# A new order of all units, with named PSUM tiles and named evacuating engines, for a fused attention and gated MLP kernel

## The chip, the cores and the metric

The kernel runs on one core of one Trainium2 chip. The metric is device time in microseconds, of one execution; several executions are timed and their median is given. The profile is of one further execution.

Engines are named as in the profile: PE is TensorE's matmul row and PEld its weight loads, DVE is VectorE, ACT is ScalarE, POOL is GpSimd, SP is the engine that issues the remaining DMAs.

## The reference, cut to what matters

```python
B, H, S, D = 4, 8, 768, 64            # q, k, v;  sort_net is [B, H, 8, 8]
P = sort_net
for _ in range(5):                    # Sinkhorn: 8x8 mixing matrices
    P = exp(P - max(P));  P /= P.sum(-1);  P /= P.sum(-2)
k_sorted[b,h,i] = sum_j P[i,j] * k[b,h,j]      # blocks of 96 rows are mixed
v_sorted[b,h,i] = sum_j P[i,j] * v[b,h,j]
attn = softmax(q_block @ k_sorted_block.T / 8) # within each block of 96
x = (attn @ v_sorted_block)                    # -> [B, 768, 512]

h = relu(x @ w_in)                    # 512 -> 1024
u, v = h[..., :512], h[..., 512:]
v_n = (v - mean(v)) / sqrt(var(v) + 1e-6)
v_s = w_spatial @ v_n + b_spatial     # mixes the 768 positions
out = (u * v_s) @ w_out               # 512 -> 512, float32
```

## The kernel before, in words

Each batch is made of **units**. A unit is a group of matmuls or transposes into one PSUM tile (two banks, 4 KB a partition; four such tiles fill PSUM) and the instruction that empties the tile.

For the attention of one batch:

- `qtr(n)`, n = 0, 1: 24 transposes of q for four heads.
- `ktr(hp)`, hp = 0..3 (a pair of heads): 12 matmuls that mix k with the diagonal matrices `pdiag` and transpose it at once (`mixed_t`, line 274). `vtr(hp)` does the same with v, and `vblk(hp)` transposes that back into blocks of 96 rows; both are used for batch 0 alone.
- `vmix(hp)`: for batches 1 to 3, two matmuls that mix v. After two of them, half of the mixed v is stored to DRAM (`vd`) and read back in blocks (`vb`) by two DMAs on SP's queue.
- `score(n)`, n = 0..7 (pair of heads n // 2, half of the blocks n % 2): 8 matmuls, and the exponential on ACT (line 324).
- `attend(n)`: 8 matmuls, then reciprocal and multiplication on DVE (lines 347, 348) into `x_sb`.
- `xtr(n)`: 16 transposes of `x_sb` into `xt`.

For the gated MLP of one batch:

- `vproj(n)`, n = 0..2: 8 matmuls of 512 columns, relu on ACT (line 389), then on DVE the statistics of two groups of rows (lines 392, 393).
- `norm`: two ACT instructions on all variances, and six normalizations on DVE (line 403).
- `uproj(mc)`, mc = 0..3: 8 matmuls of 384 columns, relu on ACT (line 419).
- `wsp_unit(gs)`, gs = 0..5: six transposes of `w_spatial`, once in the kernel, copied by DVE.
- `spatial(mc)`: 12 matmuls of 384 columns (line 428), the addition of the bias on DVE (line 434, `vs`), and the product with u on GpSimd (line 438, `gt`); the last of all has that product on DVE.
- `oproj(n)`, n = 0..2: 8 matmuls of 512 columns (line 449), the copy on ACT, and a DMA of 512 KB to the output on SP's queue.

The order of PE, DVE, ACT and GpSimd is that of the program text (`tc.manual_schedule`), so each engine takes its instructions as written. The opening is: loads, Sinkhorn, `warm(4)` (four dummy matmuls of 512 columns), both `qtr` of batch 0, `spread(0, 1)` (turns the mixing matrices of batch 0 into columns on 128 partitions: matmuls, a copy, a matmul, a copy), `make_pdiag`, `warm(2)`, and then the string `order`, which is the attention of batch 0. One step of it, `spread`, does the same for the other three batches and lets GpSimd make their `pdiag`. Then comes a loop over the four batches with one string `steps`: the gated MLP of batch b, with the attention of batch b + 1 woven in. In each turn of the loop `load` issues the loads of q, k and v of batch b + 2 on GpSimd's queue, after a copy `gate` of one element of `vb`, which holds GpSimd until that transfer has landed.

`ps_tile` draws from a pool of four buffers under one tag, so the units take the four PSUM tiles in turn:

```python
psum = ctx.enter_context(tc.tile_pool(name="psum", bufs=4, space=bass.MemoryType.PSUM))
def ps_tile(dt=FP32):
    return psum.tile([128, 2, 512 if dt == FP32 else 1024], dt, name="ps", tag="ps")
```

A unit whose turn comes to a tile that is still being emptied waits, and all of PE's later units with it. Lines 217 and 219 are the copies of the helper `copy` on ACT and on DVE.

Of the kernel before, what the change touches and what calls it, by code (L numbers as in the profile page):

```python
# [29 lines left out]
def kernel(  # L30
# [12 lines left out]
    nc = tc.nc  # L43
# [25 lines left out]
    moe_pool = ctx.enter_context(tc.tile_pool(name="moe", bufs=5))  # L69
# [16 lines left out]
    nc.sync.dma_start(out=b_nat, in_=_raw_ap(moe_b_spatial, 0, [[0, 128], [1, S]]))  # L86
# [45 lines left out]
    nc.gpsimd.dma_start(out=w_in_sb, in_=moe_w_in.rearrange("(kc p) f -> p kc f", p=128))  # L132
    wsp_nat = pers.tile([128, G, S], BF16)
# [8 lines left out]
    mask_ps = ps_tile()  # L142
# [25 lines left out]
    def warm(n):  # L168
        t = ps_tile()
        for _ in range(n):  # L170
            nc.tensor.matmul(t[:, 0, :], lhsT=ident_bf, rhs=warm_sb, start=True, stop=True)
# [4 lines left out]
    def spread(b, nb):  # L176
        n = nb * NB * H
        pt_ps = ps_tile()
        for i in range(NB):
            nc.tensor.matmul(  # L180
                pt_ps[0:NB, 0, 0:n].rearrange("p (b i h) -> p b i h", i=NB, h=H)[:, :, i, :],
                lhsT=p_bf[:, i, :], rhs=ident_bf[0:BH, b * H:(b + nb) * H],
                start=True, stop=True,
            )
        pt_sb = small.tile([NB, B * NB * H], BF16, name="pt", tag="pt")
        nc.vector.tensor_copy(out=pt_sb[:, 0:n], in_=pt_ps[0:NB, 0, 0:n])
        prep_ps = ps_tile()
        nc.tensor.matmul(prep_ps[:, 0, 0:n], lhsT=sel16, rhs=pt_sb[:, 0:n], start=True, stop=True)
        nc.vector.tensor_copy(
            out=prep_sb[:, b:b + nb].rearrange("p b i h -> p (b i h)"), in_=prep_ps[:, 0, 0:n],  # L190
        )
# [13 lines left out]
    def wsp_unit(gs):  # L205
        tp = ps_tile(BF16)
# [6 lines left out]
        nc.vector.tensor_copy(out=wspT[:, gs, :], in_=tp[:, 0, 0:S])  # L213

    def copy(eng, out, in_):
        if eng is nc.scalar:
            nc.scalar.copy(out=out, in_=in_)  # L217
        else:
            nc.vector.tensor_copy(out=out, in_=in_)  # L219

# [3 lines left out]
    class Attention:  # L224
        def __init__(self, b):
# [3 lines left out]
            self.q, self.k, self.e, self.vT = {}, {}, {}, {}  # L229

        def vmix(self, hp, eng):
            t = ps_tile()
# [12 lines left out]
            if hp == 0:  # L245
                self.vb = att.tile([BLK, NB, 2, H // 2, VW], BF16, name="vb", tag="vb")
            if hp % 2 == 1:
# [7 lines left out]
        def qtr(self, n, eng):  # L255
            t = ps_tile(BF16)
# [13 lines left out]
        def mixed_t(self, src, hp, eng):  # L270
            t = ps_tile().rearrange("p x c -> p (x c)")
# [16 lines left out]
        def ktr(self, hp, eng):  # L288
            self.k[hp] = self.mixed_t(k_in, hp, eng)


        def vtr(self, hp, eng):
            self.vT[hp] = self.mixed_t(v_in, hp, eng)

        def vblk(self, hp, eng):
            half, h0 = hp // 2, 2 * hp % (H // 2)
            if hp == 0:
                self.vb = vb0
            t = ps_tile(BF16)
# [10 lines left out]
        def score(self, n):  # L310
            hp, ih = n // 2, n % 2
            t = ps_tile()
# [17 lines left out]
        def attend(self, n):  # L330
            hp, ih = n // 2, n % 2
            if n == 0:
                self.x = att.tile([BLK, NB, DM], BF16, name="x_sb", tag="x")
            t = ps_tile()
# [20 lines left out]
        def xtr(self, n, eng):  # L355
            t = ps_tile(BF16)
# [13 lines left out]
    class Gmlp:  # L370
        def __init__(self, b):
            self.b = b
            self.v, self.u, self.gt = [], {}, []
            self.xt = [xts[b, kc] for kc in range(KC)]

        def vproj(self, n):
            t = ps_tile()
# [8 lines left out]
            if n == 0:  # L386
                self.mv = small.tile([128, G, 2], FP32, name="mv", tag="mv")
            v_sb = vsb_pool.tile([128, 2, DH], BF16, name="v_sb", tag="v")
            nc.scalar.activation(out=v_sb, in_=t, func=AF.Relu)  # L389
            for x in range(2):  # L390
# [3 lines left out]
                self.v.append(v_sb[:, x, :])  # L394

        def norm(self):
# [12 lines left out]
        def uproj(self, mc):  # L409
            t = ps_tile()  # L410
            for kc in range(KC):
# [7 lines left out]
            nc.scalar.activation(  # L419
                out=u_sb.rearrange("p (x c) -> p x c", x=2), in_=t[:, :, 0:HW], func=AF.Relu,  # L420
            )
            self.u[mc] = u_sb

        def spatial(self, mc, eng):
            t = ps_tile()
# [16 lines left out]
            self.gt.append(gt)  # L442

        def oproj(self, n, eng):
            t = ps_tile()
            for mc in range(FC):
                for x in range(2):
                    g = 2 * n + x
                    nc.tensor.matmul(  # L449
                        t[:, x, :], lhsT=self.gt[mc][:, g * 128:(g + 1) * 128],  # L450
                        rhs=w_out_sb[:, mc, :],
                        start=(mc == 0), stop=(mc == FC - 1),
                    )
            o_sb = o_pool.tile([128, 2, DM], FP32, name="o_sb", tag="o")
            copy(eng, o_sb, t)
            nc.sync.dma_start(
                out=out[self.b].rearrange("(p g) n -> p g n", g=G)[:, 2 * n:2 * n + 2, :],
                in_=o_sb,
            )

    ACT, DVE = nc.scalar, nc.vector
    with tc.manual_schedule(engines={ET.PE, ET.DVE, ET.Activation, ET.Pool}):
        a = Attention(0)
# [6 lines left out]
        order = """  # L470
            ktr0A vtr0D ktr1A vtr1A score0 vblk0D score1 ktr2D attend0 score2 attend1 score3 vblk1D
            vtr2A attend2 ktr3A attend3 score4 spread vblk2D score5 attend4 vtr3A attend5 score6
            score7 vblk3D attend6 xtr0A attend7 xtr1D
        """
        for step in order.split():
            name, rest = step.rstrip("0123456789AD"), step.lstrip("abcdefghijklmnopqrstuvwxyz")
            if name == "spread":
                spread(1, 3)
                for b in range(1, B):
                    make_pdiag(b, nc.gpsimd, 0, H)  # L480
# [4 lines left out]
            else:  # L485
                getattr(a, name)(int(rest[0]), *[{"A": ACT, "D": DVE}[e] for e in rest[1:]])
        for b in range(B):
            m = Gmlp(b)
            last = b == B - 1
            a = None if last else Attention(b + 1)  # L490
            steps = """
                vproj0 vmix0 vproj1 vmix1 vmix2 vproj2 vmix3 qtr0 norm wsp0 uproj0 ktr0 ktr1 wsp1
                uproj1 qtr1 score0 score1 wsp2 uproj2 ktr2 ktr3 wsp3 load uproj3 score2 score3
                wsp4 wsp5 spatial0 attend0 attend1 score4 score5 spatial1 attend2
                attend3 spatial2 score6 score7 attend4 attend5 spatial3 attend6 attend7 xtr0
                oproj0 oproj1 xtr1 oproj2
            """.split()
            for step in steps:
# [56 lines left out]
```

## Time and profile before

| what | value |
|---|---|
| median of 3 runs | 190.55 us (190.03 to 192.42) |
| the profiled execution | 189.82 us |
| its span, first to last instruction | 188.1 us |
| mean granted TensorE clock | 0.961 |
| PE busy | 160.3 us (85% of the span) |
| DVE busy | 108.8 us (58%) |
| ACT busy | 82.5 us (44%) |
| POOL busy | 46.9 us (25%) |
| moved by DMA | 23.92 MB, 127 GB/s over the span |

In the groups of the profile, a line gives source line, engine, operation, output and inputs with their shapes and the number of instructions, then the busy time of all of them in us, the mean of one in ns, and the idle time of the engine just before them. In the chain that ended last, a line gives the start in us from the span's start, the length, and the work. In a timeline a line begins with start and length; a number of instructions that follow each other are merged. In a window's line each engine has its busy time and number of instructions. A line of the DMA issues ends with the time from issue to landing.

### The profile page before, as it was taken

The page shows a single profiled execution, that of the slowest core. Times are in us where ns is not written, and L with a number is a line of the kernel's source. Part 1 is how long each engine was busy: PE and PEld are TensorE (multiplying, and loading weights), DVE is VectorE, ACT ScalarE, POOL GpSimd, SP SyncE. Part 2 cuts the span into 40 slices and gives each one's busy share as a digit, 9 for nine tenths or more (in the row PEclk, how much of TensorE's full clock was granted, in tenths as well). Part 3 has the DMA queues.
Part 4 walks back from the last instruction along what each step waited for, and adds up shares of the span by engine and source line. Part 5 has one row for each costly group of instructions (what it writes and reads, how often), then busy time and mean ns, then how long its engine had stood idle before and what let it go on. Part 6 is the DMA issues. An engine that isn't in the chain of part 4 may idle for free.

```text
span 188.1 us, 3963 instructions
## 1 busy us (share of the span) xinstructions
PE 160.3 (85%) x1692; PEld 102.1 (54%) x1701; DVE 108.8 (58%) x232; ACT 82.5 (44%) x107; POOL 46.9 (25%) x46
## 2 busy tenths in 40 slices
PE   1364987889889989999899899998998999999980
PEld 0062876754566666554566665545666655466430
DVE  4733386443996368726972687259726972684500
ACT  3143664435456433147566331475673315561041
POOL 7910005900000536300005463000003630003600
PEclk9999996558999999999999999999999999999998
DMA  5999999990263799152284997522810005200035
GB/s 87 161 204 209 225 202 202 204 189 3 85 173 85 84 204 204 17 223 113 98 200 55 184 204 111 223 112 90 231 27 0 3 2 223 112 3 0 0 122 213
DMA packets 21185, 23.92 MB, mean 127 GB/s; under 512 B 688, under 2 KB 18096, under 8 KB 21040
## 3 DMA queue, kind: packets, MB, share of 16 engines
q0 software_dynamic: 13680, 12.19, 41.4%
q1 hardware_dynamic: 7488, 11.49, 18.6%
q8 instruction: 13, 0.21, 0.5%
q14 instruction: 4, 0.03, 0.1%
HBM read 27.18 MB, written 8.69 MB: 191 GB/s over the span
## 4 chain that ended last, share of the span: by engine, by line
PE 55%; DVE 24%; DMA 8%; ACT 4%; POOL 4%; issue 2%; DVEq 0%; ACTq 0%; POOLq 0%
PE ps L428 15%; PE ps L381 10%; PE ps L449 9%; DMA v_in<-in_v_dram 8%; PE ps L413 7%; DVE vs L434 5%; PE ps L339 4%; DVE stats L392 3%; DVE x_sb L348 3%; PE ps L274 3%; DVE v_sb L403 3%; DVE vm L219 3%; POOL gt L438 3%; PE ps L317 2%; ACT ex L324 2%
## 5 line engine op out<-in xcount | busy, mean ns | idle before, releaser
L438 POOL TENSOR_TENSOR gt<-vs,u_sb 128x768 bf16<-128x768 f32 x15 | 24.6, 1639 | 63.7 <-DVE rec L347 41.6
L428 PE MATMUL ps<-wspT,v_sb 128*128 128x384 bf16 x192 | 33.4, 326 | 1.6 <-ACT ex L324 1.6
L324 ACT ACTIVATE ex<-ps 96x768 bf16<-96x768 f32 x32 | 24.4, 803 | 23.4 <-PE ps L317 23.4
L434 DVE TENSOR_TENSOR vs<-ps,b_bc 128x768 f32<-128x768 f32 x16 | 15.3, 958 | 19.9 <-PE ps L428 19.8
L217 ACT COPY o_sb<-ps 128x1024 f32<-128x1024 f32 x12 | 12.1, 1012 | 33.1 <-PE ps L449 33.1
L428 PEld LDWEIGHTS <-v_sb 128*128 128x128 bf16 x192 | 18.3, 98 | 12.9 <-issue 1.7
L392 DVE BATCH_NORM_STATS2 stats<-v_sb 128x6 f32<-128x512 bf16 x24 | 16.2, 676 | 15.5 <-ACT v_sb L389 15.5
L381 PE MATMUL ps<-w_in_sb,xt 128*128 128x512 bf16 x92 | 23.6, 397 | 0.8 <-DVE xt L219 0.6
L449 PE MATMUL ps<-w_out_sb,gt 128*128 128x512 bf16 x92 | 22.5, 380 | 1.6 <-POOL gt L438 0.7
L413 PE MATMUL ps<-xt,w_in_sb 128*128 128x384 bf16 x128 | 23.0, 326 | 1.0 <-DVE kT L219 0.8
L348 DVE TENSOR_TENSOR x_sb<-ps,rec 96x512 bf16<-96x512 f32 x32 | 22.0, 687 | 1.1
L339 PE MATMUL ps<-vb,ex 96*96 96x65 bf16 x256 | 16.4, 217 | 2.1 <-DVE vb L219 1.7
L339 PEld LDWEIGHTS <-ex 96*96 96x96 bf16 x256 | 15.4, 133 | 4.2 <-issue 2.1
L389 ACT ACTIVATE v_sb<-ps 128x1024 bf16<-128x1024 f32 x12 | 12.3, 1023 | 10.9 <-PE ps L381 10.9
L413 PEld LDWEIGHTS <-w_in_sb 128*128 128x128 bf16 x128 | 12.0, 97 | 8.7 <-issue 1.1
L419 ACT ACTIVATE u_sb<-ps 128x768 bf16<-128x768 f32 x16 | 12.6, 806 | 8.1 <-PE ps L413 8.1
L381 PEld LDWEIGHTS <-xt 128*128 128x128 bf16 x96 | 9.6, 101 | 12.0 <-DVE xt L219 1.1
L449 PEld LDWEIGHTS <-gt 128*128 128x128 bf16 x96 | 8.6, 98 | 12.5 <-POOL gt L438 2.7
L219 DVE CAST kT<-ps 128x768 bf16<-128x768 f32 x8 | 7.7, 956 | 8.8 <-PE ps L274 8.8
L217 ACT CAST kT<-ps 128x768 bf16<-128x768 f32 x12 | 9.5, 796 | 6.5 <-PE ps L274 6.5
L262 PE MATMUL ps<-ident_bf,q_in 128*64 128x128 bf16 x192 | 7.9, 244 | 4.8 <-DMA q_in<-in_q_dram 4.4
L506 POOL COPY gate<-vb 1x1 bf16<-1x1 bf16 x2 | 0.4, 178 | 45.5 <-DMA vb<-vd 45.5
(72 smaller groups left out, 176.9 us busy)
## 6 DMA issues: line engine op xcount, KB each, us to landing
out_dram<-o_sb SPq DMA_DIRECT2D x12, 512.0 KB, 2.6
q_in<-in_q_dram POOLq DMA_DIRECT2D x4, 768.0 KB, 10.6
k_in<-in_k_dram POOLq DMA_DIRECT2D x4, 768.0 KB, 13.9
v_in<-in_v_dram POOLq DMA_DIRECT2D x4, 768.0 KB, 11.1
vd<-vm SPq DMA_DIRECT2D x6, 390.0 KB, 3.0
vb<-vd SPq DMA_DIRECT2D x6, 390.0 KB, 4.3
wsp_nat<-in_moe_w_spatial_dram POOLq DMA_DIRECT2D x1, 1152.0 KB, 23.2
w_in_sb<-in_moe_w_in_dram POOLq DMA_DIRECT2D x1, 1024.0 KB, 18.6
```

The source lines that it names most:

```text
L217: nc.scalar.copy(out=out, in_=in_)
L219: nc.vector.tensor_copy(out=out, in_=in_)
L324: nc.scalar.activation(out=e.rearrange("p h i c -> p h (i c)"), in_=t[0:BLK, :, 0:NB // 2 * BLK], func=AF.Exp, scale=scale,)
L339: nc.tensor.matmul(t[0:BLK, hh, ii * VW:(ii + 1) * VW], lhsT=self.e[n][:, hh, ii, :], rhs=self.vb[:, i, h // (H // 2), h % (H // 2), :], s ...
L348: nc.vector.tensor_mul(out=self.x[:, ih * (NB // 2):(ih + 1) * (NB // 2), hp * 128:hp * 128 + 128] .rearrange("p i (h d) -> p h i d", h=2) ...
L381: nc.tensor.matmul(t[:, x, :], lhsT=self.xt[kc][:, g * 128:(g + 1) * 128], rhs=w_in_sb[:, kc, DH:DFF], start=(kc == 0), stop=(kc == KC - 1),)
L392: nc.vector.bn_stats(out=stats, in_=v_sb[:, x, :])
L413: nc.tensor.matmul(t[:, x, 0:HW], lhsT=w_in_sb[:, kc, mc * 128:(mc + 1) * 128], rhs=self.xt[kc][:, x * HW:(x + 1) * HW], start=(kc == 0), ...
L428: nc.tensor.matmul(t[:, x, 0:HW], lhsT=self.v[g][:, mc * 128:(mc + 1) * 128], rhs=wspT[:, g, x * HW:(x + 1) * HW], start=(g == 0), stop=(g ...
L434: nc.vector.tensor_add(out=vs, in0=t[:, :, 0:HW], in1=b_bc.rearrange("p (x c) -> p x c", x=2),)
L438: eng.tensor_mul(out=gt.rearrange("p (x c) -> p x c", x=2), in0=vs, in1=self.u[mc].rearrange("p (x c) -> p x c", x=2),)
L449: nc.tensor.matmul(t[:, x, :], lhsT=self.gt[mc][:, g * 128:(g + 1) * 128], rhs=w_out_sb[:, mc, :], start=(mc == 0), stop=(mc == FC - 1),)
```

## The change

The strings `order` and `steps` go, and with them the loop over batches. One string, `SCHEDULE`, lists every unit of the whole kernel. Each word has five signs: the unit, its number, its batch, the engine that empties the tile (A for ACT, D for DVE, - where there is no choice), and the number of its PSUM tile. The tiles are four tags with one buffer each.

- In the opening, `b_nat` (the bias) is loaded on GpSimd's queue behind `w_in` instead of on SP's at the start; `warm(4)` becomes `warm(9)`, `spread` is cut in two with one dummy matmul between, and `warm(2)` becomes `warm(4)`.
- In the attention of batch 0 the `spread` for the other batches comes first, then all `ktr` with the first scores, then all `vtr`, `vblk`, and the rest. Four of the six `wsp` units are done before the first `vproj`.
- In the middle stages `vproj`, `vmix`, `uproj`, `qtr` and `ktr` alternate, three of the four `uproj` come before or among the scores, `norm` comes after the third `uproj`, and the attends follow the scores at some distance. `spatial` runs in the order 2, 0, 1, 3 or 1, 2, 0, 3.
- `uproj` and `wsp` can be emptied by either engine, and so are `vblk` and `oproj`.
- The gate is now two copies, one for each half of `vb`, and the loads come at the first `spatial` of a batch.
- In the last batch, `oproj` finishes one half of its tile and then the other; DVE copies the first half and ACT the second, each with its own store.
- Buffers: `qk` 5 to 7 (for k), `ex` 4 to 6, `moe` 5 to 4.

```diff
-    qk_pool = ctx.enter_context(tc.tile_pool(name="qk", bufs=5))
-    ex_pool = ctx.enter_context(tc.tile_pool(name="ex", bufs=4))
+    qk_pool = ctx.enter_context(tc.tile_pool(name="qk", bufs=7))
+    ex_pool = ctx.enter_context(tc.tile_pool(name="ex", bufs=6))
...
-    psum = ctx.enter_context(tc.tile_pool(name="psum", bufs=4, space=bass.MemoryType.PSUM))
-    def ps_tile(dt=FP32):
-        return psum.tile([128, 2, 512 if dt == FP32 else 1024], dt, name="ps", tag="ps")
+    psum = ctx.enter_context(tc.tile_pool(name="psum", bufs=1, space=bass.MemoryType.PSUM))
+    def ps_tile(n, dt=FP32):
+        return psum.tile(
+            [128, 2, 512 if dt == FP32 else 1024], dt, name=f"ps{n}", tag=f"ps{n}",
+        )
...
-    nc.sync.dma_start(out=b_nat, in_=_raw_ap(moe_b_spatial, 0, [[0, 128], [1, S]]))
...
     nc.gpsimd.dma_start(out=w_in_sb, in_=moe_w_in.rearrange("(kc p) f -> p kc f", p=128))
+    nc.gpsimd.dma_start(out=b_nat, in_=_raw_ap(moe_b_spatial, 0, [[0, 128], [1, S]]))
...
+    def relu(eng, out, in_):
+        if eng is nc.scalar:
+            nc.scalar.activation(out=out, in_=in_, func=AF.Relu)
+        else:
+            nc.vector.tensor_scalar(out=out, in0=in_, scalar1=0.0, scalar2=None, op0=ALU.max)
...
+            pairs = [(mc, x) for mc in range(FC) for x in range(2)]
+            if self.last:
+                pairs = [(mc, x) for x in range(2) for mc in range(FC)]
...
+            if self.last:
                 for x in range(2):
+                    copy(DVE if x == 0 else ACT, o_sb[:, x, :], t[:, x, :])
+                    nc.sync.dma_start(out=o_dram[:, x, :], in_=o_sb[:, x, :])
...
+    SCHEDULE = """
+        P00-0 k00A1 k10A2 R00-3 s00-0 k20D1 s20-3 k30D2 s10-0 t00D1 t30A3 t20D2 t10A0 s70-1
+        B00D3 B30D2 B10A0 p00-1 B20A3 p10-2 s30-0 p20-1 p70-3 s60-2 s40-0 p30-1 s50-2 p60-3
+        p40-0 x00A1 p50-2 w20D3 w50D0 x10D1 w30D2 w10D3 V00-0 v11A1 V10-2 w40D3 V20-0 v31A1
+        U20A2 v01D0 w00A3 U10A1 v21D2 k31A3 q01D0 k01A1 k11D2 q11D3 k21A0 U30D1 N00-- s31-2
+        s61-0 U00A3 s51-1 s11-2 S20-0 s41-3 s71-1 S00-2 a61-0 a41-3 S10-1 a51-2 a71-0 S30-3
+        s01-1 s21-2 x11D0 a31-1 a11-3 a01-2 O00A0 a21-1 O20A3 x01D2 O10A0 V01-1 v02D3 v32A2
+        V21-0 v22A1 V11-2 v12A0 U11A3 k32A1 q02D2 k02A0 q12D3 k12A1 k22A2 U21D0 N01-- s02-3
+        s32-1 U31A2 s62-0 s22-3 S11-1 s12-2 s42-0 U01D3 a22-1 S21-2 a42-0 a32-3 S01-1 a02-2
+        a12-0 S31-3 s52-1 s72-2 x02D0 a62-1 a52-3 O01A2 a72-0 O11A1 x12D3 O21D2 V02-0 v03D1
...
+        s03-1 s33-0 U32A3 s63-2 s23-1 S12-0 s13-3 s43-2 U02D1 a23-0 S22-3 a43-2 a33-1 S02-0
+        a03-3 a13-2 S32-1 s53-0 s73-3 x03D2 a63-0 a53-1 O02A3 a73-2 O12A0 x13D1 O22D3 V03-2
+        V23-0 V13-1 U13A3 U23D2 N03-- U33A0 S13-1 U03D3 S23-2 S03-0 S33-1 O03A3 O13A2 O23D0
+    """
+    UNITS = {
+        "v": "vmix", "k": "ktr", "q": "qtr", "s": "score", "a": "attend", "p": "attend",
+        "x": "xtr", "t": "vtr", "B": "vblk",
+        "V": "vproj", "N": "norm", "U": "uproj", "S": "spatial", "O": "oproj",
+    }
...
-        warm(4)
-        a.qtr(0, ACT), a.qtr(1, ACT)
-        spread(0, 1)
+        warm(9, 1)
+        attn[0].qtr(0, ACT, 2), attn[0].qtr(1, ACT, 3)
+        spread_t(0, 1, 0), warm(1, 1)
+        spread(0, 1, 0)
         make_pdiag(0, DVE, 0, 2), make_pdiag(0, DVE, 2, 6)
-        warm(2)
+        warm(4, 1)
...
+                if name == "S":
+                    if not gmlp[b].gt and b + 2 < B:
                         gate = small.tile([1, 2], BF16, name="gate", tag="gate")
+                        for x in range(2):
+                            nc.gpsimd.tensor_copy(
+                                out=gate[:, x:x + 1], in_=attn[b + 1].vb[0:1, 0, x, 0, 0:1],
+                            )
                         v_in[b + 2] = load_heads(v, b + 2, "v_in")
                         q_in[b + 2] = load_heads(q, b + 2, "q_in")
                         k_in[b + 2] = load_heads(k, b + 2, "k_in")
```

In `SCHEDULE`, P and R are the two halves of `spread` for batches 1 to 3 (`spread_t` and `spread`), p is an `attend` of batch 0, w is a `wsp` unit, and the other letters are those of `UNITS`.

More of the change, by code (lines that the diff above doesn't have):

```diff
@@ L484 @@
                 )
[L485 to L498, printed above, removed]
[L499 to L504 removed]
+            elif name == "w":
+                wsp_unit(n, eng, ps)
+            elif name in "VNUSO":
+                if b not in gmlp:
+                    gmlp[b] = Gmlp(b)
+                if name == "S":
+                    if not gmlp[b].gt and b + 2 < B:
                         gate = small.tile([1, 2], BF16, name="gate", tag="gate")
[L506 removed]
+                        for x in range(2):
+                            nc.gpsimd.tensor_copy(
+                                out=gate[:, x:x + 1], in_=attn[b + 1].vb[0:1, 0, x, 0, 0:1],
+                            )
                         v_in[b + 2] = load_heads(v, b + 2, "v_in")
```

190 lines of the change are left out of this document (86 added, 104 removed).

## The prediction, made before the changed kernel was run

> **What bounds the kernel now.** I read the page's first part, then the chain that ended last in order of time, then the windows and the groups. On the page:
>
> ```profile
> span 188.1 us, 3963 instructions
> PE 160.3 (85%) x1692; PEld 102.1 (54%) x1701; DVE 108.8 (58%) x232; ACT 82.5 (44%) x107; POOL 46.9 (25%) x46
> ```
>
> PE is far ahead of the rest, so either its work or the gaps in it set the time. The chain shows where each batch's first `vproj` starts (line 381), and so the length of each stage:
>
> ```profile
> 41.27 2.62 PE ps L381 x6
> ...
> 83.12 1.73 PE ps L381 x8
> ...
> 120.88 1.73 PE ps L381 x8
> ...
> 158.67 2.37 PE ps L381 x11
> ```
>
> The opening (attention of batch 0) lasts 41.3 us; the stages of batches 0, 1 and 2 last 41.85, 37.76 and 37.79; the last takes 188.1 - 158.67 = 29.4. What must PE do in a middle stage? Pieces of the chain that run on into the next PE piece give prices without the drain of the last matmul:
>
> ```profile
> 69.24 0.71 PE ps L339 x16
> ...
> 98.17 0.79 PE ps L274 x24
> ...
> 100.37 0.49 PE ps L317 x16
> ...
> 118.47 0.68 PE ps L361 x16
> ...
> 124.66 0.65 PE ps L235 x4
> ...
> 163.85 5.20 PE ps L413 x32
> 169.05 7.81 PE ps L428 x48
> ```
>
> Per batch: 3 `vproj` and 3 `oproj` at 1.73 (8 matmuls of 512 columns both) 10.4; 4 `uproj` 5.2; 4 `spatial` 7.8; 4 `vmix` at 0.65/2 1.3; 4 `ktr` at 0.79/2 1.6; 2 `qtr` (24 matmuls of the same shape each) 1.6; 8 `score` at 0.49/2 2.0; 8 `attend` at 0.71/2 2.8; 2 `xtr` 1.4. Sum **34.1 us**, against 37.8: PE stands still for 3.7 us a stage. The chain says where:
>
> ```profile
> 93.86 1.94 DVE v_sb L403 x6
> 95.79 0.88 DVE kT L219
> 96.71 1.46 PE ps L413 x8
> ...
> 100.86 2.06 PE ps L428 x12
> ```
>
> The page gives the prices of what empties PSUM and of VectorE's other work:
>
> ```profile
> L438 POOL TENSOR_TENSOR gt<-vs,u_sb 128x768 bf16<-128x768 f32 x15 | 24.6, 1639 | 63.7 <-DVE rec L347 41.6
> ...
> L324 ACT ACTIVATE ex<-ps 96x768 bf16<-96x768 f32 x32 | 24.4, 803 | 23.4 <-PE ps L317 23.4
> ...
> L434 DVE TENSOR_TENSOR vs<-ps,b_bc 128x768 f32<-128x768 f32 x16 | 15.3, 958 | 19.9 <-PE ps L428 19.8
> ...
> L392 DVE BATCH_NORM_STATS2 stats<-v_sb 128x6 f32<-128x512 bf16 x24 | 16.2, 676 | 15.5 <-ACT v_sb L389 15.5
> ...
> L348 DVE TENSOR_TENSOR x_sb<-ps,rec 96x512 bf16<-96x512 f32 x32 | 22.0, 687 | 1.1
> ...
> L389 ACT ACTIVATE v_sb<-ps 128x1024 bf16<-128x1024 f32 x12 | 12.3, 1023 | 10.9 <-PE ps L381 10.9
> ...
> L419 ACT ACTIVATE u_sb<-ps 128x768 bf16<-128x768 f32 x16 | 12.6, 806 | 8.1 <-PE ps L413 8.1
> ```
>
> After `vproj` VectorE has three pairs of `bn_stats`/`bn_aggr` (about 1.55 a pair of groups), two `vmix` copies, the copy of `qtr0`, six normalizations (1.94) and the copy of `ktr1` in a row. The four PSUM tiles go round in order, so PE queues behind whichever tile VectorE has not emptied. To see whether prices and waits alone explain this I walked the old order of batch 1 by hand: a unit starts when PE is free, its tile is empty and its operands are there; each engine evacuates in the written order, 0.15 to 0.2 after the unit's last matmul. I get `spatial0` at 17.85 after `vproj0`; the chain has 100.86 - 83.12 = 17.74. I trust the walk to a few tenths a stage.
>
> **The change, the middle stages.** No matmul is added to them; they get another order, named tiles and named engines. The new order of batch 1 by the same walk, as PE start / tile empty, in us after `V0`: V0 0/2.9, v0 1.7/5.4, v3 2.1/3.7, V2 2.4/5.3, v2 4.1/6.1, V1 4.4/7.4, v1 6.2/8.2, U1 6.5/9.0, k3 7.8/9.8, q0 8.2/10.0, k0 8.9/10.6, q1 9.2/11.1, k1 9.9/11.4, k2 10.3/12.2, U2 10.6/13.1, normalization 13.1 to 15.0, s0 11.9/13.5, s3 12.2/14.3, U3 12.4/15.1, s6 13.7/15.9, s2 14.0/16.7, S1 14.4/17.5, s1 16.3/17.5, s4 16.6/18.3, U0 16.8/19.3, a2 18.1/20.1, S2 18.5/21.6, a4 20.4/22.4, a3 20.8/23.2, S0 21.1/24.3, a0 23.1/25.1, a1 23.5/25.9, S3 23.8/27.0, s5 25.8/27.0, s7 26.1/27.8, x0 26.3/28.1, a6 27.1/29.0, a5 27.4/29.8, O0 27.9/30.8, a7 29.6/31.0, O1 30.0/32.9, x1 31.7/33.5, O2 32.4, next V0 at **34.1**. Almost no wait is left; the tightest are k1 and U2, whose tiles come free with 0.1 or less to spare, and a6, which waits 0.05. `normalization` now stands behind four score and projection units of PE, so its 1.94 no longer stops anything. Batch 2 is the same order with the tiles renamed. I take 34.3 for each.
>
> `uproj` on VectorE isn't in the trace: bounded by the 0.806 that ScalarE takes for it and the 0.958 of L434, same input; I take 0.95, nearer in engine. In batch 1 two of them and one `oproj` copy (bounded by ScalarE's 1.02 for such a tile and 0.958 x 1024/768, taken 1.2) move 3.1 to VectorE; two `ktr` and one `vmix` copy move 2.8 off it. A first-half `wsp` copy on ScalarE I bound by 0.55 (VectorE) and 0.80 (L324's size) and take 0.8; `vblk` there by 0.80 and 1.44 (0.80 for 768 elements, 1.44 for 1536), 1.0. None stands on PE's path unless its tile comes within 0.1.
>
> **The moved loads.** The gate and the loads of the batch after next go from before `uproj3` to the first `spatial`, the gate now with two copies, one for each half of `vb`:
>
> ```profile
> vd<-vm SPq DMA_DIRECT2D x6, 390.0 KB, 3.0
> vb<-vd SPq DMA_DIRECT2D x6, 390.0 KB, 4.3
> ...
> wsp_nat<-in_moe_w_spatial_dram POOLq DMA_DIRECT2D x1, 1152.0 KB, 23.2
> ```
>
> The last `vmix` half is out of PSUM at 8.2 (batch 1), 11.1 (batch 0); with 3.0 + 4.3 and the issue, `vb` stands at 16 and 18.8. Behind the gate on GpSimd: three DMA issues (that of `wsp`, in the timeline below, takes 0.55; I count 0.9 for each of these, which are cut into more pieces), then the first `gt` (1.64). In batch 0 that `gt` ends near 23.7, just as VectorE's third `vs` wants its buffer (two bufs); in batch 1 there are 2 us to spare. The first `attend` wants `vb` at 20.9 in batch 0 and 18.1 in batch 1. So batch 0 is at the edge: each us that the bounce is late costs up to one there.
>
> **Batch 0.** My walk gives 34.85 with two of the six `wsp` units left in it (34.1 + 0.9 of work). Its start runs at half clock, below, as it did before from 41.27 to about 43; half the length of a stretch is lost, and for 3 us I add 1.5: **36.3**.
>
> **The opening.** `b_nat` leaves SP's queue for GpSimd's, behind `w_in`. What it took from `q`:
>
> ```profile
> q1 hardware_dynamic: 92, 0.23, 41.9%
> ```
>
> That is the window 3 to 6 us: 42% of 3 us, 1.3 us. (It started before q's first packets, at no cost.) q lands at 9.4, not 10.7, k and v 1.3 sooner too, v at 17.1; `wsp` and all behind it are unmoved, since the same bytes stay ahead of them, and `b_bc` is wanted only by the first `spatial`. `sinkhorn` is as before and ends ahead of q's transposes. The timeline of the opening:
>
> ```profile
> 6.24 0.55 POOL L134 DMA_DIRECT2D wsp_nat<-in_moe_w_spatial_dram  x1
> ...
> 10.68 2.77 PE L262 MATMUL ps<-ident_bf,q_in 128*64 128x128 bf16 x48 [4.38 <-DMA q_in<-in_q_dram]
> ...
> 14.53 1.29 DVE L196 TENSOR_TENSOR pdiag<-mask,prep_sb 128x256 bf16<-128x256 bf16 x2
> ...
> 15.12 0.85 PE L274 MATMUL ps<-pdiag,k_in 128*64 128x128 bf16 x12 [0.36 <-DVE pdiag L196]
> ```
>
> With q 1.3 sooner and one dummy ahead of `spread`, `pdiag` moves from 14.5 to 13.4. But four dummies (0.43 each at half clock) and `spread_t(1,3)` now stand between `spread` and `ktr0`, so `ktr0` starts at 15.2, no sooner than before. What is gained comes after: the `k` and score units fill PE while v loads, where it idled to 18.4, and no unit waits long. How fast it then goes depends on the clock:
>
> ```profile
> 18.41 2.13 PE ps L274 x36
> ...
> 32.63 0.78 PE ps L339 x8
> 33.41 0.81 PE ps L317 x16
> 34.22 1.03 PE ps L301 x8
> ...
> 36.79 1.28 PE ps L361 x16
> ```
>
> ```profile
> PE   1364987889889989999899899998998999999980
> ...
> PEclk9999996558999999999999999999999999999998
> ```
>
> (A slice is 4.7 us.) At 18.4 us 36 matmuls take 59 ns each, at 98.2 us 33 ns: PE ran at half there although the row says 9, and the row has it at half again from about 30 to 43, until after `vproj` has begun, with PE busy at 8 tenths; only some 7 of the 26 us were full. At half clock, with the drain taken off these rows, the opening's eight k and v units (0.65), eight scores (0.41), four `vblk` (0.93), eight `attend` (0.75), two `xtr` (1.3), four `wsp` (0.7) and the rest are some 24 us of PE: `vproj` at 39.3. At full clock VectorE and ScalarE bound it, and the last wait is `wsp` (6.24 + 23.2 + 0.4 for the longer queue = 29.8, estimate), then two `wsp` units, `xtr1` and its copy (0.5 + 0.5 + 0.7 + 0.95): `vproj` at 32.4. The full-clock walk does in 13.2 us, from `ktr0` to the last `attend`, what takes 19.6 at half; so one full stretch of 7 us, as before, saves 3.3 of the 39.3: I take **36.0**, with four `wsp` units (1.9) already done. The old value is 41.27.
>
> [...]
>
> **The last stage.** PE's 18.2 us to the end of `spatial` stay (my walk: 18.4). Then 0.96 + 0.96 on VectorE, as now. `oproj` of the last batch goes half by half, so it stops after three matmuls, not six, and 21 of 0.216 remain, not 18: +0.65. The last copy,
>
> ```profile
> 183.13 1.01 ACT o_sb L217
> ```
>
> becomes a half one, bounded by 0.5 and 1.0, taken 0.57: -0.45; its store is half as large, worth 0 to -0.6. Three more issues on SP hide behind matmuls. Sum about nothing: **29.4**.
>
> **Sum.** 36.0 + 36.3 + 34.3 + 34.3 + 29.4 = 170.3 of span. The profiled execution took 189.82 for 188.1 of span; its 1.7 around gives 172.0. The median shown is 0.4% above that execution, so I say **172.5**.
>
> **Rivals.**
> 1. *Full clock through the opening* (`vproj` at 32.4, no 1.5 in batch 0): 5.1 less, 167.4. For it: nine 512-wide dummies. Against: the half clock from 30 to 43. [...] 0.10.
> 2. *The order slips.* With four tiles used to within 0.1 us, one late evacuation or late `vb` passes down the whole order; GpSimd's gate holds `gt`. If half of each stage's gain goes (1.8 in three stages) and the opening stays at half clock (3.3): 181. Against: the walk's match of the old order. 0.17.
> 3. *The gaps aren't gaps*: PE is 85% busy, and matmuls packed closer stretch, because weight loads no longer hide. The stages stay at 37.8 and the opening's `attend` chain on VectorE too: about 188. Against: the prices above were taken where PE ran dense. 0.04.
> 4. *Slower: the clock.* If small units mixed among the wide ones keep PE at half from the opening through batch 0 and on, each 2 us so spent lose 1. It decides at 36 us of half clock more than I count, half of what batch 0 would then last; all of batch 0 at half would give about 205. For it: 30 to 43 at half with PE busy. Against: the row is at 9 from there to the end with the same mix of units. 0.03.
>
> My forecast has the remaining 0.66. Range **167 to 179**: rival 1 to most of rival 2, leaving out 3, 4 and the far end of 2. About 2% (3.8 us) is what a measurement can tell from no change: faster 0.93, same 0.04, slower 0.03.
>
> **What would show it.** `vproj` starts at 36, 72, 107 and 141; about 34.3 between the last three; `ktr0` still at 15; q's transposes from 9.4; no run of VectorE pieces ahead of `uproj` in the chain; the last stage 29.4. I am wrong if the middle stages stay above 36, or if the granted clock is half beyond the opening.

## The result, and the profile after

| | before | changed |
|---|---|---|
| median | 190.29 us (4 runs, 188.96 to 192.42) | **169.59 us** (4 runs, 168.18 to 171.38) |
| profiled execution | 189.82 us | 168.18 us |
| its span | 188.1 us | 166.4 us |

The ratio is **0.891**, 95% interval 0.881 to 0.900: 11% faster. The forecast was 172.5, range 167 to 179. Ratios here leave out executions that stand apart from the fastest of their kernel; in the first set of experiments they therefore compare with two executions of the old kernel at 185.1 and 186.4 us, well below its median.

From the page of the changed kernel, its span, the busy time of the engines, and two rows of 40 slices (4.2 us each): PE's busy tenths and its granted clock.

```profile
span 166.4 us, 3983 instructions
...
PE 152.2 (91%) x1709; PEld 95.9 (58%) x1709; DVE 114.0 (69%) x236; ACT 79.7 (48%) x106; POOL 47.9 (29%) x49
...
PE   0979993999999999999999999999999999999680
...
PEclk9999999699999999999999999999999999999999
```

PE has one hole, in the seventh slice, and one slice of lower clock behind it; from there until far into the last stage it is at 9. The chain that ended last (start, length, work) has the ends of the stages:

```profile
6.81 22.15 DMA wsp_nat<-in_moe_w_spatial_dram
...
29.00 0.87 PE ps L217 x12
...
32.03 2.58 PE ps L396 x8
...
67.85 1.73 PE ps L396 x8
...
102.14 1.73 PE ps L396 x8
...
136.43 1.74 PE ps L396 x8
```

L396 is `vproj` and L217 a `wsp` unit. The opening is 32.0 us, the stages are 35.8, 34.3, 34.3 and 30.0. Of the 21.7 us between the two profiled spans, 9.2 lie in the opening, 13.0 in the first three stages (6.0, 3.5 and 3.5), and the last stage is 0.5 longer. The opening hangs on the landing of `w_spatial`. Inside a middle stage the chain is nothing but PE, one unit behind the other; where VectorE's row of statistics, copies and normalizations stood, there is now

```profile
78.43 1.41 PE ps L428 x8
79.84 0.49 PE ps L332 x16
80.33 1.41 PE ps L428 x8
81.73 0.49 PE ps L332 x16
82.22 2.06 PE ps L441 x12
```

that is `uproj`, two scores, `uproj`, two scores and the first `spatial`, 14.4 us after `vproj` instead of 17.7. (In batches 1 and 2 `norm` comes after the second `uproj`; only in batch 0 after the third.)

### The profile page after: what moved, and what is told of

It is laid out like the page before. It is cut to its first block, busy times and chain, and to the rows that moved or that the text cites. A ratio compares the mean times of both kernels' runs of the same rounds, so it can differ in the third digit from the quotient of the medians.

```text
span 166.4 us, 3983 instructions
## 1 busy us (share of the span) xinstructions
PE 152.2 (91%) x1709; PEld 95.9 (58%) x1709; DVE 114.0 (69%) x236; ACT 79.7 (48%) x106; POOL 47.9 (29%) x49
## 4 chain that ended last, share of the span: by engine, by line
PE 74%; DMA 13%; DVE 5%; POOL 3%; issue 1%; ACT 1%; DVEq 0%; POOLq 0%
PE ps L441 19%; DMA wsp_nat<-in_moe_w_spatial_dram 13%; PE ps L464 12%; PE ps L396 11%; PE ps L428 11%; PE ps L354 5%; PE ps L332 4%; PE ps L376 3%; PE ps L291 3%; PE ps L279 2%; PE ps L251 2%; DVE stats L407 2%; PE ps L217 2%; DVE mv L408 1%; ACT v_sb L232 1%
## 5 line engine op out<-in xcount | busy, mean ns | idle before, releaser
L441 PEld LDWEIGHTS <-v_sb 128*128 128x128 bf16 x192 | 17.6, 98 | 11.9 <-DVE v_sb L418 1.5
L396 PE MATMUL ps<-w_in_sb,xt 128*128 128x512 bf16 x96 | 23.3, 390 | 0.0
L232 ACT ACTIVATE v_sb<-ps 128x1024 bf16<-128x1024 f32 x12 | 12.3, 1024 | 18.7 <-PE ps L396 18.7
L226 ACT COPY o_sb<-ps 128x1024 f32<-128x1024 f32 (+1 forms) x10 | 8.8, 884 | 25.9 <-DVE o_sb L228 15.0
L428 PEld LDWEIGHTS <-w_in_sb 128*128 128x128 bf16 x128 | 11.8, 98 | 7.8
L396 PEld LDWEIGHTS <-xt 128*128 128x128 bf16 x96 | 9.6, 101 | 10.9 <-issue 0.8
L354 PEld LDWEIGHTS <-ex 96*96 96x96 bf16 x256 | 14.3, 125 | 2.0
L354 PE MATMUL ps<-vb,ex 96*96 96x65 bf16 x256 | 14.8, 209 | 0.1
L226 ACT CAST kT<-ps 128x768 bf16<-128x768 f32 x15 | 11.5, 799 | 2.5 <-PE ps L291 2.4
L228 DVE COPY xt<-ps 128x1536 bf16<-128x1536 bf16 x7 | 6.7, 959 | 5.3 <-PE ps L376 5.3
L332 PEld LDWEIGHTS <-kT 64*96 64x96 bf16 x256 | 7.4, 121 | 4.7 <-issue 3.5
L234 DVE TENSOR_SCALAR u_sb<-ps 128x768 bf16<-128x768 f32 x7 | 6.7, 953 | 4.8 <-PE ps L428 4.8
```

The costliest lines, as they stand in the source:

```text
L332: nc.tensor.matmul(t[0:BLK, hh, ii * BLK:(ii + 1) * BLK], lhsT=self.k[hp][rows, i * BLK:(i + 1) * BLK], rhs=self.q[hp][rows, i], start=Tru ...
L354: nc.tensor.matmul(t[0:BLK, hh, ii * VW:(ii + 1) * VW], lhsT=self.e[n][:, hh, ii, :], rhs=self.vb[:, i, h // (H // 2), h % (H // 2), :], s ...
L396: nc.tensor.matmul(t[:, x, :], lhsT=self.xt[kc][:, g * 128:(g + 1) * 128], rhs=w_in_sb[:, kc, DH:DFF], start=(kc == 0), stop=(kc == KC - 1),)
L428: nc.tensor.matmul(t[:, x, 0:HW], lhsT=w_in_sb[:, kc, mc * 128:(mc + 1) * 128], rhs=self.xt[kc][:, x * HW:(x + 1) * HW], start=(kc == 0), ...
L441: nc.tensor.matmul(t[:, x, 0:HW], lhsT=self.v[g][:, mc * 128:(mc + 1) * 128], rhs=wspT[:, g, x * HW:(x + 1) * HW], start=(g == 0), stop=(g ...
```

## The experiments

My theory was that the stages shrink because the new order and the new engines keep VectorE from holding PSUM tiles that PE wants, and that the opening shrinks because it ran at full clock up to the landing of `w_spatial`. The rivals: the dummies do it, the naming of tiles does it, the engines alone do it, the order alone does it. Three sets were run, each beside the kernel before (medians 189.59, 189.89 and 191.71). The changed kernel itself ran again in the third set alone (170.40 us), so kernels of the first two sets are compared with 169.59 from another set; a difference of 1 or 2 us is therefore read from the lengths of the stages in the traces, one execution each, and not from the medians.

**The old numbers of dummies.**

```diff
-        warm(9, 1)
+        warm(4, 1)
...
-        spread_t(0, 1, 0), warm(1, 1)
+        spread_t(0, 1, 0)
...
-        warm(4, 1)
+        warm(2, 1)
```

> The changed kernel with the old numbers of dummy matmuls (4 at the start, none in the middle of spread, 2 after pdiag, instead of 9, 1 and 4). Theory A, the dummies carry the clock through the opening: half clock there again, the first vproj at 36 to 39 us instead of 32, 173 to 176 us. Rival B, the denser order carries the clock by itself, or the landing of w_spatial at 29 us hides what half clock costs: vproj still at 32 to 33, 169 to 171 us.

Measured: 168.27 us, ratio 0.905 (0.895 to 0.914): rival B, in its second form, though 0.7 below the range that I gave it. Its timeline on PE:

```profile
8.67 2.77 PE L279 MATMUL ps<-ident_bf,q_in 128*64 128x128 bf16 x48 [2.55 <-DMA q_in<-in_q_dram]
...
13.50 1.49 PE L291 MATMUL ps<-pdiag,k_in 128*64 128x128 bf16 x24
...
27.58 0.51 PE L354 MATMUL ps<-vb,ex 96*96 96x65 bf16 x8
29.29 1.42 PE L217 MATMUL ps<-ident_bf,wsp_nat 128*128 128x128 bf16 x12 [1.20 <-DMA wsp_nat<-in_moe_w_spatial_dram]
```

and of the changed kernel:

```profile
8.67 2.02 PE L279 MATMUL ps<-ident_bf,q_in 128*64 128x128 bf16 x48 [0.40 <-DMA q_in<-in_q_dram]
...
13.49 1.00 PE L291 MATMUL ps<-pdiag,k_in 128*64 128x128 bf16 x24
...
25.94 0.51 PE L354 MATMUL ps<-vb,ex 96*96 96x65 bf16 x8
...
29.00 0.87 PE L217 MATMUL ps<-ident_bf,wsp_nat 128*128 128x128 bf16 x12 [2.55 <-DMA wsp_nat<-in_moe_w_spatial_dram]
```

The dummies do what they are there for: with them 24 `ktr` matmuls take 1.00 us, without them 1.49, and the last `attend` of the opening is 1.6 us sooner. But both kernels then stand and wait for `w_spatial`; most of the 1.6 us goes into a longer wait (2.55 us against 1.20). In its chain `vproj` starts at 33.1, 1.1 later than in the changed kernel, because the units behind that wait run slower here (1.42 us against 0.87 for the 12 transposes); stage 0 is 0.9 shorter, and the spans are 166.6 and 166.4. So the end of the opening hangs on `w_spatial`, and not on the dummies as I thought.

**The new numbers of dummies in the old order.** `warm(4)` to `warm(9)`, `warm(2)` to `warm(4)`, one dummy in `spread`; nothing else of the old kernel is changed.

> The kernel before with the new numbers of dummies (9, 1, 4) and nothing else. Theory A, the dummies carry the clock: full clock from about 9 us to 30, the first vproj 2 to 4 us sooner, 186.5 to 188.5 us. Rival B, the old opening is bounded by the landing of v (18.4 us) and the chain of vblk and attend on VectorE, not by PE's clock: within 1 us of before, 189.5 to 190.5.

Measured: 191.27 us, median of before 189.59, ratio 1.029 (1.017 to 1.041). No gain in any case: rival B, or a little worse. The page of its trace shows that full clock isn't held:

```profile
PEclk9978695556999999999999999999999999999999
```

It goes up and down through the opening: 0.71 from 10 to 15 us, 0.84, 0.76 and 0.92 in the next three stretches of 5 us, and 0.50 from 30 to 45. In its timeline PE idles for 3.15 us behind the dummies, until q lands, and for 2.61 us until v lands. So in the old order the dummies bring nothing; that the clock itself is worth something there is in the last section. Together with the run before, this leaves the rest of what was changed there as what shortened the opening (41.3 to 32.0 us): the order, its engines, and the place of the bias, which a run below takes back. Order and engines were not tried apart in the opening.

**The old order in the stages.** The opening and the last stage are those of the changed kernel; `SCHEDULE` has, from `V00` to `V03`, the old `steps` for each batch, with tiles 0, 1, 2, 3 in turn, the old engines and the old place of `load`.

```diff
-  V00-0 v11A1 V10-2 w40D3 V20-0 v31A1 U20A2 v01D0 ...
+  V00-0 v01A1 V10-2 v11D3 v21A0 V20-1 v31D2 q01D3 N00-- w00D0 U00A1 k01A2 k11D3 U10A0 ...
```

> The new opening and the new last stage, with the old order, the old engines, tiles in turn and the old place of the loads in the stages of batches 0 to 2 (four of the six wsp units stay in the opening). Theory A, the parts add up: stage 0 at 40.0 instead of 35.8 (41.85 less 1.9 of moved wsp units), stages 1 and 2 at 37.8 instead of 34.3, 181 us. Rival B, part of the shorter stages comes from how the opening hands over (clock, loads already landed): stage 0 nearer 37, 177 to 178 us.

Measured: 183.2 us, median of before 189.59, ratio 0.987 (0.974 to 1.001). Stage starts in its chain:

```profile
74.88 1.73 PE ps L396 x8
...
112.95 1.73 PE ps L396 x8
...
151.42 1.74 PE ps L396 x8
```

The first of these is the start of batch 1; that of batch 0 in this chain is 34.3. Stages 0, 1 and 2 take 40.5, 38.1 and 38.5 us, where 40.0, 37.8 and 37.8 were expected, so theory A holds for the stages. The span is 15.0 us longer than that of the changed kernel (181.4 - 166.4): 12.7 lie in the three stages and 2.3 in the opening, which is the same program in both but ran at half clock at its end, for 6.9 us here by the mean clock of the execution (0.981 over 181.4 us) and for 3.4 us there. The median is 2.2 us above the expected 181, and by its interval the new opening alone is not told apart from executions of the old kernel at full clock.

**Four buffers under one tag instead of names.**

```diff
-    psum = ctx.enter_context(tc.tile_pool(name="psum", bufs=1, space=bass.MemoryType.PSUM))
+    psum = ctx.enter_context(tc.tile_pool(name="psum", bufs=4, space=bass.MemoryType.PSUM))
...
-            [128, 2, 512 if dt == FP32 else 1024], dt, name=f"ps{n}", tag=f"ps{n}",
+            [128, 2, 512 if dt == FP32 else 1024], dt, name="ps", tag="ps",
```

> The changed kernel with the four PSUM tiles taken in turn, as before, in the new order. Theory A, by the hand walk of batch 1 the tiles are nearly in turn anyway; only vproj1 would wait for the tile of vmix0, which VectorE empties late (about 1 us a stage in batches 1 and 2, less in batch 0): 171 to 172.5 us. Rival B, the naming is the point, since every late tile then blocks the order: 2 us a stage or more, 175 us and up. Rival C, the order alone does it: 169.6 within 0.7.

Measured: 169.78 us, ratio 0.906 (0.892 to 0.921). From its chain:

```profile
71.63 0.65 PE ps L396 x3
...
105.92 0.65 PE ps L396 x3
...
140.21 0.65 PE ps L396 x3
```

34.29 and 34.29, to 0.01 the stages of the changed kernel. The naming is worth nothing: rival C. But the pool does not hand out its buffers strictly in turn, as I had taken it to. In turn, `vproj1` (the third `vproj` of the batch) would come to the tile of `vmix0`, four units before it. In this trace it starts before VectorE begins to empty that tile:

```profile
75.90 1.89 PE L396 MATMUL ps<-w_in_sb,xt 128*128 128x512 bf16 x8
...
76.08 0.93 DVE L228 CAST vm<-ps 128x768 bf16<-128x768 f32 x1
```

So it has another tile. My 1 us a stage was for a strict rotation, which this run does not have, and what that would cost in the new order was not measured. So "in turn" is not shown for the kernel before either, which has the same pool.

**The old engines in the new order.** Words of `SCHEDULE` from `V00` on, 26 changed, for example

```diff
-  v02D3 v32A2 V21-0 v22A1 V11-2 v12A0 U11A3 k32A1 q02D2 ... U21D0
+  v02A3 v32D2 V21-0 v22A1 V11-2 v12D0 U11A3 k32D1 q02D2 ... U21A0
```

> The changed kernel with the new order and the named tiles, but from the first vproj on with the old engines (uproj and oproj on ScalarE, vmix and ktr with even numbers on ScalarE and with odd ones on VectorE, wsp on VectorE): 26 units of the stages change hands. Theory A, the engine of each unit is chosen for the order: by the hand walk of batch 1 PE waits for the tiles of vmix3 (1.0 us), vmix1 (1.0), qtr0 (0.5) and the score tiles, and the first spatial comes 3 us later than in the changed kernel; 34.3 becomes about 37 a stage, 177 to 179 us. Rival B, the order alone does it: 169 to 171 us.

Measured: 177.68 us, with a median of 189.89 for before. Its chain in batch 1:

```profile
70.50 1.74 PE ps L396 x8
...
75.03 0.85 DVE vm L228
75.92 1.90 PE ps L396 x8
...
87.95 2.11 PE ps L441 x12
...
107.92 1.73 PE ps L396 x8
```

Theory A to the place: PE waits for the copy of a `vmix` on VectorE, behind the statistics, before the third `vproj`; the first `spatial` comes at 17.45 instead of 14.4, and the stage lasts 37.4, as do the two around it.

**The new engines in the old order.** The kernel with the old order, with 23 units on their new engines.

> The kernel of the third experiment (new opening, old order in the stages, tiles in turn) with the new engine of each unit (23 units change hands). Theory A, engines and order only work together: by the hand walk of batch 1 vmix0 and two uproj on VectorE now stand behind bn_stats and the normalization, and the first spatial comes 18.7 us after vproj0, not 17.9: 183 to 186 us. Rival B, the engines are worth 2.7 us a stage in any order, as they are in the new one: 175 to 177 us.

Measured: 182.77 us, ratio 0.955 (0.948 to 0.963); its pair, with the old engines, had 183.2. From its chain:

```profile
72.19 1.74 PE ps L396 x8
...
76.72 0.85 DVE vm L228
...
91.44 2.07 PE ps L441 x12
...
111.39 1.73 PE ps L396 x8
```

The first `spatial` comes at 19.3 (I had walked to 18.7) and the stage lasts 39.2, longer than with the old engines. So the engines pay only in the new order: a middle stage takes 38.1 to 38.5 with neither, 39.2 with the new engines alone, 37.4 with the new order alone, and 34.3 with both. In the medians, across the sets, new engines alone gain 0.4 us, the new order with the old engines 5.5 (183.2 to 177.7), of which by the traces 3.1 lie in stage 0, and both together 13.6 (to 169.6). The new order includes the new place of the loads. The larger buffers (`qk`, `ex`) were in all these kernels: with the old order they bring nothing, and whether the new order needs them was not run.

**The bias first, and last.** In the one the load of `b_nat` goes back to SP's queue at the start; in the other it goes behind all loads of the start.

```diff
     nc.gpsimd.dma_start(out=w_in_sb, in_=moe_w_in.rearrange("(kc p) f -> p kc f", p=128))
-    nc.gpsimd.dma_start(out=b_nat, in_=_raw_ap(moe_b_spatial, 0, [[0, 128], [1, S]]))
```

> The changed kernel with the bias loaded on SP's queue at the start again, ahead of q. Theory A, the opening is bounded by the landing of w_spatial (29.0 us), and the bytes ahead of that are the same: q lands 2 us later (10.7), the first vproj stays at 32, 169 to 170.5 us. Rival B, the chain from q on sets the end of the opening: 2 us later, 171 to 172.5 us.

> The changed kernel with the load of the bias moved behind all other loads of the start. Theory A, PE's 2.55 us of idling for w_spatial are bytes: 384 KB less ahead of it at about 200 GB/s, so it lands 1.7 us sooner (27.3), the first vproj at 30.3, 167 to 168 us. Rival B, other waits of the opening (the last attend on VectorE, xtr1, its copy) take up the place: less than 0.6 gained, 169 to 170.

Measured: 168.47 us with the bias first, 167.71 with the bias last, with 189.89 for before in the same set. With the bias first:

```profile
9.94 1.53 PE L279 MATMUL ps<-ident_bf,q_in 128*64 128x128 bf16 x48 [1.68 <-DMA q_in<-in_q_dram]
...
28.87 1.48 PE L217 MATMUL ps<-ident_bf,wsp_nat 128*128 128x128 bf16 x12 [1.73 <-DMA wsp_nat<-in_moe_w_spatial_dram]
```

q lands 1.3 us later than in the changed kernel, and it costs nothing that can be seen: `w_spatial` still lands at 28.9, and in the chain `vproj` starts at 32.6 (32.0 in the changed kernel). That is theory A; the median is 0.5 below its range. With the bias last:

```profile
27.75 0.87 PE L217 MATMUL ps<-ident_bf,wsp_nat 128*128 128x128 bf16 x12 [1.30 <-DMA wsp_nat<-in_moe_w_spatial_dram]
...
29.81 2.01 PE L396 MATMUL ps<-w_in_sb,xt 128*128 128x512 bf16 x8
```

`w_spatial` lands 1.25 us sooner (I expected 1.7), and in this view `vproj` starts at 29.8 instead of 31.8. In that trace the gain is then given back: in the chain stage 0 takes 39 us (29.98 to 69.00), for the reason that follows; the gate on GpSimd opens 21.7 us after the first `vproj`.

**The loads between the products.** In some executions stage 0 is longer than 35.8. The changed kernel was run again in the third set:

> The changed kernel once more, beside the kernels of this set, as what they are compared with: 168 to 171 us.

Measured: 170.40 us, ratio 0.890 (0.883 to 0.897). Its chain in stage 0, which begins at 33.4:

```profile
55.47 0.18 POOL gate L533
...
55.97 0.86 POOL v_in L93
...
58.68 1.68 POOL gt L451
...
60.39 0.96 DVE vs L447
...
71.34 1.73 PE ps L396 x8
```

The gate opens at 55.5, 22 us after the first `vproj`; in the first trace it was 19.6. GpSimd stands at its gate until then, issues three loads in 2.7 us, and only then makes its first `gt`. The third `vs` on VectorE waits 2.38 us for the buffer that this `gt` frees; behind it PE waits three times, 0.41, 0.45 and 0.46 us, for a tile that `vs` or an `attend` empties late or for `x_sb`. Stage 0 lasts 37.9. Against the 35.0 of the last kernel below, 1.0 of it is the first `vproj` at half clock (2.72 us instead of 1.73). The edit puts the v load with its gate behind the first `gt`, q behind the second, k behind the third:

```diff
+                if name == "S" and b + 2 < B:
+                    done = len(gmlp[b].gt)
+                    if done == 1:
...
+                        v_in[b + 2] = load_heads(v, b + 2, "v_in")
+                    elif done == 2:
+                        q_in[b + 2] = load_heads(q, b + 2, "q_in")
+                    elif done == 3:
+                        k_in[b + 2] = load_heads(k, b + 2, "k_in")
```

> The changed kernel with GpSimd's gate and v load behind the first gt of a stage, the q load behind the second and the k load behind the third, instead of all ahead of the first. Theory A, in stage 0 the gate (which waits for vb) and the three issues (2.7 us) hold GpSimd's four gt (6.6 us), and oproj waits where vb lands late (gate open 20.7 us after the first vproj in one trace, 19.6 in another): stage 0 at 35.6 in every execution, 167.5 to 168.7 us. Rival B, oproj waits for something else: 169 to 170. Rival C, v of the next batch but one now lands too late for the first vmix of the next stage (it is wanted 37.5 us after the first vproj): 170 to 172.

Measured: 168.81 us, ratio 0.881 (0.875 to 0.887), 1.6 us less than the changed kernel beside it. Its timeline and chain:

```profile
52.81 1.64 POOL L451 TENSOR_TENSOR gt<-vs,u_sb 128x768 bf16<-128x768 f32 x1 [27.46 <-ACT ex L339]
54.39 0.30 POOL L537 COPY gate<-vb 1x1 bf16<-1x1 bf16 x2
```

```profile
68.16 1.73 PE ps L396 x8
```

The gate no longer waits, and stage 0 (from 32.85) takes 35.3. The loads came soon enough (the next stage takes 34.3): rival C is out. The median is 0.1 above what I expected.

**Another end of the last batch.** Each half of an `oproj` gets its own PSUM tile and output tile; the matmuls of the first three `gt` run for three halves while the last `gt` is made.

```diff
+            for g, ps in ((0, 3), (1, 2), (2, 0)):
+                part(g, 1, ps), part(g, 2)
+            for g in range(3):
+                part(g, 0)
+            for g in range(3):
+                part(g, 3), done(g)
+            for g, ps in ((3, 1), (4, 3), (5, 2)):
+                part(g, 1, ps), part(g, 2), part(g, 0), part(g, 3), done(g)
```

> The changed kernel with another end of the last batch: each half of an oproj has its own PSUM tile and its own output tile, the matmuls of gt 1, 2 and 0 for three halves are done while the last gt is made, so 15 matmuls remain behind it and not 21, and each half is copied as soon as its four matmuls are done, by VectorE and ScalarE in turn. Theory A, after the last gt 6 matmuls less (1.3 us) and one half copy less in a row at the end (0.7): the last stage 28.0 instead of 30.0, 167.3 to 168 us. Rival B, the copies go on waiting for each other, whatever tile they write: 168.2 to 168.7.

Measured: 167.77 us (189.89 for before in that set). The last stage takes 165.9 - 137.5 = 28.4 instead of 30.0. In its timeline the copies overlap, and the last one waits for PE and no longer for VectorE:

```profile
158.19 3.41 PE L480 MATMUL ps<-w_out_sb,gt 128*128 128x512 bf16 x15 [0.24 <-DVE gt L451]
158.62 1.29 DVE L228 COPY o_half<-ps 128x512 f32<-128x512 f32 x2 [0.48 <-PE ps L480]
158.83 0.59 ACT L226 COPY o_half<-ps 128x512 f32<-128x512 f32 x1 [11.31 <-PE ps L480]
...
161.63 0.59 ACT L226 COPY o_half<-ps 128x512 f32<-128x512 f32 x1 [1.14 <-PE ps L480]
```

That is theory A, by 1.6 of the 2.0 that I expected. From the last `gt` to the end of the last copy all of the 2.0 is saved (4.1 us instead of 6.1), but from there to the end of the span it takes 3.7 us and not 3.25; why the last store ends later stays open. Both the PSUM and the output tile were parted, so which of the two made the copies wait isn't told apart.

**All three together**: bias last, loads between the products, the other end.

> The bias last, the other end of the last batch and the loads between the gt, together. Theory A, they add: 1.7 at the opening, 1.9 at the end, about 1 in stage 0 from 169.6: 164.5 to 165.7 us. Rival B, with the opening 1.7 shorter the mixed v of batch 1 goes out and back while the first loads still run, and what the opening gains is lost to the wait for vb in stage 0: 166 to 167.5.

Measured: **165.0 us**, ratio 0.862 (0.856 to 0.868), beside 170.4 for the changed kernel: 5.4 us less. The parts add: in its chain the opening is 31.3 us, stage 0 35.0 and the last stage 28.4, against 33.4, 37.9 and 30.0 in the trace beside it. Stage 0 keeps what the opening gains, so rival B is out. This version beats both kernels.

## Why the prediction was right, point by point

- **The middle stages**: 34.3 forecast, 34.29 measured, twice. The sum over PE's units and the walk by hand, with prices of the old trace, both gave 34.1 and were good to 0.2 us; the 0.2 that I put on top had no reason given, so that it fits to 0.01 is luck. The walk with the old engines was good to 0.4 (37 against 37.4), the one with the new engines in the old order to 0.6 (`spatial` at 18.7 against 19.3). The walk with tiles in turn was for a rotation that did not take place.
- **What had held PE**: VectorE behind `vproj`, as read from the chain. Order and engines each had to move to free it; the prediction didn't say how much each was worth, and took the named tiles as a part of it, which they aren't. That the old tiles "go round in order" isn't shown either.
- **Batch 0**: 36.3 forecast, 35.8 in the profiled execution. The walk's 34.85 was right (35.0 where nothing disturbs it); the 1.5 for half clock was too much, since only the first `vproj` lost by it, 0.85 (2.58 us instead of 1.73). The edge that was named, `vb` landing late behind GpSimd's gate, is real: 37.9 in another trace. Of the 3.5 us between the two traces of the changed kernel, 2.1 lie in stage 0 and 1.4 in the opening.
- **The opening** is the mis-sized term: 36.0 forecast, 32.0 measured, and rival 1, with a chance of 0.10, said 32.4. I had one stretch of 7 us at full clock. In the changed kernel the clock was full from the middle of q's transposes to 30 us, some 20 us (its row has 1.00 from 9.7 to 30.2). From `ktr0` to the end of the last `attend` it took 13.0 us; the walk had 13.2 at full clock. The last wait was the landing of `w_spatial`, at 29.0 against an estimated 29.8. `ktr0` began at 13.5, not 15.2: the four dummies before it took 1.04 us, not 1.7, and q landed at 8.7, not 9.4. With the old dummies, and some 10 us at full clock ahead of the landing of `w_spatial` (eight matmuls of a score took 0.55 us at 17.78 and 0.38 at 20.17), `vproj` still began at 33.1.
- **What full clock was worth.** With the nine dummies q's 48 transposes take 2.02 us, with four 2.77. That dummies keep the clock full through the opening, as rival 1 has it, was an assumption that no trace of before shows. The time of the kernel doesn't hang on them, since the old dummies give the same total (168.27 us against 169.59). And in the old order the new dummies didn't hold the clock (0.71 from 10 to 15 us, 0.50 from 30 to 45).
- **The last stage**: 29.4 forecast, 30.0 measured. `gt` was ready at 20.6 and 21 matmuls remained, as counted. The chain then shows what went wrong:

```profile
157.09 4.72 PE ps L464 x21
...
161.84 0.70 DVE o_sb L228
...
162.56 0.59 ACT o_sb L226
```

  The half copy on VectorE starts after the whole tile is done, and ScalarE's starts after VectorE's: 1.31 us in a row where I had 0.57. The smaller last store gave 0.7 back (3.25 us from the end of the copy to the end of the span, 3.96 before).
- **The sum**: 4.0 too much in the opening, 0.5 too much in batch 0, 0.6 too little in the last stage: 170.3 against 166.4. The median, 169.6, lies nearer to rival 1's 167.4 than to the 172.5 of the forecast: the stages came out as forecast, the opening as rival 1 had it, though the dummies that rival 1 goes by were not what did it. Rivals 2, 3 and 4 did not happen; of rival 2 only the piece with GpSimd's gate did, in some executions.

## What to carry to other kernels

Add up what the bounding engine must do in a stage, from pieces of the chain that run on without a wait; if the stage is much longer, walk the order by hand with the prices of the trace, engine by engine, and see whose tile is late. An order and the engines that empty its tiles have to be changed together: in a middle stage either alone brought at most 1 us of 4 here, or lost 1. After such a change look at what the freed engine now waits for (here bytes ahead of one load, and a gate at the head of an in-order engine), because that is where the next microseconds are.

## What the runs showed of the hardware

- The old kernel's time goes with the mean clock of the execution. The same program had a mean clock of 1.00 and 184.8 to 186.4 us, 0.95 to 0.96 and 188.3 to 191.7, or 0.92 and 190.6 to 193.9; in its one trace (0.961) the record has it below full only from 30.0 to 43.7 us and at the very end. The changed kernel's were 0.974 to 0.99, with 168.2 to 171.7. So part of the 11% is time that most executions of the old kernel lose at half clock; against the three old executions at full clock the gain is about 8.5%. What decides the clock of one execution stays open.
- In the old kernel's trace the clock was half for 13.65 us, from 30.0 to 43.7 us, with PE busy for 11.8 of 13.6 us, up to 40.0 in small matmuls. In the changed one's it was half for 3.41 us, from 30.2 us, after PE had idled for 2.55 us up to 29.0. Idling doesn't settle it: with the bias last PE idled for 1.30 us at that place and the clock stayed full (the 12 transposes behind it took 0.87 us), with all three parts together it idled for 1.09 us and the clock fell (1.48 us for them, and a mean of 0.75 from 25 to 30 us).
- In the old trace the clock row says full (1.00) from the start to 30.0 us, and for the first part of that it isn't to be trusted: 12 of the k matmuls took 0.85 us at 19.05 with the row at full, as long as 12 of the same shape at 31.8 with the row at half; at 25.5 they took 0.53.
- A copy of 512 float32 elements a partition out of PSUM took 0.69 us on VectorE and 0.59 on ScalarE; `uproj`'s relu on VectorE took 0.953, as bounded.
